# A fused attention, expert and bilinear kernel: the order of its first expert phase, its conversions and its weight buffers changed

## The chip, the cores and the metric

The kernel runs on one core of one Trainium2 chip. A core has five engines that each work through their own list of instructions in order and wait for each other by semaphores: TensorE (PE, matrix products), VectorE (DVE), ScalarE (ACT), GpSimd (POOL) and SyncE (SP), which here only issues transfers. SBUF is the working memory that all engines read, PSUM the banks into which TensorE adds its products. The metric is the time of one execution on the device in microseconds, lower is better.

## What is computed

Three layers follow each other, all in float32.

```python
# 1. attention with decay: B=2, H=8, S=768, D=64, blocks of 64
intra = (q_b @ k_b.T * Dmask) @ v_b
inter = (q_b * lam**(pos+1)) @ kv_state
x[block] = intra + inter              # then x: 1536 x 512
# 2. four experts, each token weighted with p
for e in range(4):
    h = np.maximum(x @ w1[e], 0.0)    # 512 -> 1024
    out += p[:, e:e+1] * (h @ w2[e])  # 1024 -> 512
# 3. bilinear
a = x @ w1; b = x @ w2                # 512 -> 1024 each
y = ((a * b) @ w3) @ w_out            # 1024 -> 1024 -> 512
```

The weights of the third layer come as 64-bit numbers and are turned into float32 on the chip.

## The kernel before

**Precision.** Each float32 operand is split into a high part (rounded, a copy on ScalarE, line 102, names ending in h) and a low part (the difference, a subtraction on VectorE, line 105, names ending in l). A product is then three matmuls: high by low, low by high, high by high (`products`, line 122).

**Stages.** The 1536 tokens are three groups of 512. First comes the attention, with the first expert columns laid between its steps by a list written by hand (`ORDER`). Then **phase one**: for group 0 a loop over the columns k = 8 to 31 (an expert has eight columns of 128 hidden features). Each column is twelve matmuls h, then z (relu times probability, VectorE, line 318, reads the bank of h), hh and hl (its split, lines 325 and 331), and twelve matmuls y of the column k-2. Then **phase two**: groups 1 and 2 together in sixteen chunks m of two columns each, with seven products of sums instead of eight (`multiply`, line 776), for which the weights are summed too (`pair_sums`, lines 682 to 685). Last come the gates and the output.

**What is laid between the columns of phase one.** Calls are put down by `at_step(t, rank, ...)` with a number t = 100 * column + place; `step(t)` issues all that are due, four times a column: after the first six matmuls of h (place 0), after z and hh (25), after half of y (50), after hl (75). Sorting is by t, then by rank. Nothing else sets the order: each engine takes its instructions as they are issued. These are:

- the weights of the column j to come: `prep_high(j)`, `prep_low(j)` (names wh, wl; 1024 wide), in slots s0, s1, ...; a load of the next column is issued when the low part is done with its raw tile;
- the conversion of the 64-bit weights in pieces i = 0 to 23 (w_out 0 to 7, w3 8 to 23; tiles cv): `begin64` (two operations on ScalarE, lines 201 and 205), `bits64` (three on VectorE, lines 211, 215 and 220, then one addition on GpSimd, line 227), `end64` (the split into wo or w3, h and l). The load of the piece i+3 needs the raw tile that the addition of piece i has read;
- `w_block`: W = w3 @ w_out is computed ahead, in one PSUM bank (7): four blocks of six matmuls for each of eight rows kt, then `w_sum` copies the bank (ScalarE, line 614) and `w_store` sends it to DRAM;
- `x_sums` and `x_split`: sums of groups 1 and 2 and their splits, for phase two;
- the early pair sums: `early_load` (line 692) brings the weights of a chunk into a tile of which there is one, `pair_sums` works in it, `early_store` (line 695) sends it to DRAM, from where phase two takes it (t_dram). This is done for the first NPRE chunks; the others make their sums in phase two.

Of the kernel before, what the change touches and what calls it, by code (L numbers as in the profile page):

```python
# [14 lines left out]
P = 128  # L15
# [45 lines left out]
def tile_decay_attention__then__moe_relu__then__bilinear(  # L61
# [73 lines left out]
    def slot_of(j):  # L135
        return j if j < 8 else (j - 8) % 5
# [101 lines left out]
    def end64(i, low):  # L238
# [10 lines left out]
        elif what == "w3":  # L249
            half = q  # L250
            if "w3" not in slots:
                slots["w3"] = pair(1024, "s7", "w3")
            to = slots["w3"]
# [335 lines left out]
    early = ExitStack()  # L589
    wo_p = opened(early, "wo")  # L590
    xs_p = opened(early, "xs")
    ws_p = opened(early, "ws", 2)
    ct_p = opened(early, "ct", 3)
# [5 lines left out]
    def w_block(kt, q, half):  # L599
        if q == 0 and half == 0:  # L600
# [3 lines left out]
                cut("w3", q * 512 + m * P, q * 512 + (m + 1) * P),  # L604
# [42 lines left out]
    NPRE = 8  # L647
# [239 lines left out]
    for j in range(10, NJ):  # L887
        at_step(100 * (j - 3) + 60, 0, None, lambda j=j: prep_high(j))
        at_step(100 * (j - 3) + 76, 0, ("j", j), lambda j=j: prep_low(j))
    for i in range(24):  # L890
        what, n, q, _ = f64[i]
        t = 808 + 95 * i if i < 8 else 1568 + 68 * (i - 8)
        at_step(t, 3, None, lambda i=i: begin64(i))
        at_step(t + 50, 2, None, lambda i=i: bits64(i))
        at_step(t + 75, 9, ("f", i), lambda: None)
        at_step(t + 125, 3, None, lambda i=i: end64(i, False))
        at_step(t + 150, 4, None, lambda i=i: end64(i, True))
        if what == "w3":
            at_step(t + 225, 6, None, lambda n=n, q=q: w_block(n, q, 0))
            at_step(t + 250, 6, None, lambda n=n, q=q: w_block(n, q, 1))  # L900
            if q:
                at_step(t + 251, 1, None, lambda n=n: w_sum(n))
                at_step(t + 325, 9, None, lambda n=n: w_store(n))
    for i, (n, d) in enumerate((n, d) for n in (3, 1, 2, 4) for d in range(2)):
        at_step(1800 + 50 * i, 7, None, lambda n=n, d=d: x_sums(n, d))
    for t, key, src, hi, lo in (
        (2200, "a11", lambda: x_block(0, 0), "xh10", "xh20"),
        (2300, "a12", lambda: x_block(0, 1), "xh11", "xl10"),
        (2400, "a22", lambda: x_block(1, 1), "xh21", "xl20"),
        (2500, "s4", lambda: x_sum[4], "xl11", "xl21"),  # L910
        (2900, "s2", lambda: x_sum[2], "s5h", "s5l"),
        (2925, "s1", lambda: x_sum[1], "s7h", "s7l"),
        (2950, "s3", lambda: x_sum[3], "s6h", "s6l"),
# [3 lines left out]
    for n in range(NPRE):  # L917
        t = 1800 + 120 * n
# [521 lines left out]
```

## Time and profile before

| what | value |
|---|---|
| median of 3 runs | 803.81 us (803.28 to 804.42) |
| profiled execution, its own time | 803.04 us |
| its span from first to last instruction | 801.3 us |
| TensorE busy | 788.7 us (98%) |
| VectorE busy | 554.0 us (69%) |
| ScalarE busy | 332.2 us (41%) |
| GpSimd busy | 148.9 us (19%) |
| mean granted clock of TensorE | 0.998 |

The profile is of one execution. A busy time is the sum of an engine's instructions as the profiler saw them; matmuls overlap each other, so the time from one start to the next says more than the length of one. Idle time of an engine counts only where the engine that ends last waits for it.

### The profile page before, as it was taken

Reading aid. Unit: us, or ns where it says so; the run is one execution under the profiler, and the core shown is the slowest. Engines: PE = TensorE matmul, PEld = TensorE weight load, DVE = VectorE, ACT = ScalarE, POOL = GpSimd, SP = SyncE. Lnnn points to the kernel's source line nnn. Section 1 sums busy time; section 2 is a strip of 40 time slices with the busy share of each in tenths; the row PEclk is TensorE's granted clock in tenths of the full one; section 3 lists DMA queues with packets and bytes.
Section 4 is the critical chain, followed back from the end, with each engine's and each line's share of the span. In section 5 each row is a group of like instructions: output and inputs, shape, how many; then the busy total and the mean of one; then the engine's idle time right before and its main releaser. Section 6 shows DMA issues by size and latency. Waiting matters only on the chain.

```text
span 801.3 us, 10423 instructions
## 1 busy us (share of the span) xinstructions
PE 788.7 (98%) x3968; PEld 645.3 (81%) x3968; DVE 554.0 (69%) x835; ACT 332.2 (41%) x570; POOL 148.9 (19%) x107
## 2 busy tenths in 40 slices
PE   9999999999899999999999999999999999999998
PEld 7777888777777888888888888888888888888887
DVE  7654499998985577667677878787856777677400
ACT  4543256454552465534443334433344442444301
POOL 2112032232220001110001111111100521677000
PEclk9999999999999999999999999999999999999999
DMA  8794356676754165343423232322234201000011
GB/s 268 250 318 141 132 180 198 224 247 207 261 177 148 61 186 175 118 132 114 126 102 106 92 106 93 105 93 92 92 106 145 79 26 54 1 0 1 1 52 53
DMA packets 44418, 101.40 MB, mean 127 GB/s; under 512 B 4944, under 2 KB 10320, under 8 KB 44368
## 3 DMA queue, kind: packets, MB, share of 16 engines
q1 hardware_dynamic: 43696, 100.70, 37.9%
q8 instruction: 31, 0.51, 0.2%
q14 instruction: 19, 0.16, 0.1%
q10 hardware_dynamic: 672, 0.03, 0.1%
HBM read 86.01 MB, written 14.70 MB: 126 GB/s over the span
## 4 chain that ended last, share of the span: by engine, by line
PE 80%; DVE 12%; DMA 5%; issue 1%; ACT 1%; SPq 0%; POOL 0%; ACTq 0%; DVEq 0%; POOLq 0%
PE y L122 27%; PE h L776 19%; PE o L122 8%; PE h L122 5%; PE ab L122 5%; PE a L1236 5%; PE b L1236 5%; DMA w<-in_w_dram 3%; DVE wl L105 2%; PE a L525 2%; PE a L442 2%; DVE hl L331 2%; PE a L519 1%; PE w L122 1%; DVE w3l L105 1%
## 5 line engine op out<-in xcount | busy, mean ns | idle before, releaser
L122 PE MATMUL y<-zp,w 128*128 128x512 f32 x768 | 186.3, 389 | 0.0
L122 PEld LDWEIGHTS y<-zp,w 128*128 128x128 f32 x768 | 144.0, 188 | 30.3 <-ACT ya L855 0.2
L227 POOL TENSOR_TENSOR cv<-cv,raw 128x512 uint32<-128x512 uint32 x40 | 71.3, 1782 | 434.2 <-DVE cv L220 402.2
L796 ACT CAST zp<-z 128x512 fp32r<-128x512 f32 x64 | 39.8, 622 | 107.8 <-DVE z L791 107.8
L325 ACT CAST hh<-z 128x512 fp32r<-128x512 f32 x32 | 19.9, 621 | 106.1 <-DVE z L318 106.1
L122 PE MATMUL o<-w_hi,z 128*128 128x512 f32 (+1 forms) x208 | 60.1, 373 | 0.2 <-DVE z L105 0.2
L800 DVE TENSOR_TENSOR zp<-z,zp 128x512 fp32r<-128x512 f32 x64 | 44.1, 689 | 17.9 <-ACT zp L796 16.5
L105 DVE TENSOR_TENSOR wl<-raw,wh 128x1024 fp32r<-128x1024 f32 (+1 forms) x33 | 41.4, 1253 | 15.8 <-ACT wh L102 15.8
L122 PE MATMUL h<-xl,wh 128*128 128x512 f32 x128 | 51.2, 400 | 0.0
L122 PE MATMUL y<-hl,wh 128*128 128x512 f32 x128 | 50.5, 394 | 0.0
L122 PE MATMUL h<-xh,wl 128*128 128x512 f32 x128 | 50.0, 391 | 0.0
L122 PE MATMUL y<-hh,wl 128*128 128x512 f32 x128 | 49.9, 389 | 0.0
L122 PE MATMUL y<-hh,wh 128*128 128x512 f32 x128 | 49.8, 389 | 0.0
L122 PEld LDWEIGHTS o<-w_hi,z 128*128 128x128 f32 x208 | 37.9, 188 | 7.4 <-DVE z L105 0.5
L789 DVE TENSOR_TENSOR z<-h,v 128x512 f32<-128x512 f32 x16 | 11.0, 690 | 43.5 <-ACT wf L102 29.4
L105 DVE TENSOR_TENSOR w<-w,w 128x512 fp32r<-128x512 f32 x32 | 31.2, 975 | 12.0 <-ACT w L102 12.0
L122 PE MATMUL o<-w_lo,z 128*128 128x512 f32 (+1 forms) x104 | 38.2, 373 | 0.0
L102 ACT CAST wh<-raw 128x1024 fp32r<-128x1024 f32 (+1 forms) x33 | 33.7, 1020 | 9.4 <-PE y L122 5.1
L318 DVE SCALAR_TENSOR_TENSOR z<-h,pb 128x512 f32<-128x512 f32 x32 | 21.9, 685 | 18.8 <-PE h L122 18.3
L122 PE MATMUL h<-xh,wh 128*128 128x512 f32 x128 | 34.8, 390 | 0.0
L791 DVE SCALAR_TENSOR_TENSOR z<-z,pb 128x512 f32<-128x512 f32 x48 | 33.2, 692 | 1.7
L331 DVE TENSOR_TENSOR hl<-z,hh 128x512 fp32r<-128x512 f32 x32 | 28.8, 900 | 5.2 <-ACT hh L325 5.2
(227 smaller groups left out, 1666.9 us busy)
## 6 DMA issues: line engine op xcount, KB each, us to landing
w<-in_w_dram SPq DMA_DIRECT2D x40, 512.0 KB, 4.2
raw<-in_w_dram SPq DMA_DIRECT2D x31, 512.0 KB, 4.4
raw<-in_w3t_dram SPq DMA_DIRECT2D x16, 512.0 KB, 3.3
raw<-in_wab_dram SPq DMA_DIRECT2D x16, 512.0 KB, 3.4
raw<-in_wout_dram SPq DMA_DIRECT2D x8, 512.0 KB, 3.8
t_dram<-w SPq DMA_DIRECT2D x8, 512.0 KB, 3.0
t<-t_dram SPq DMA_DIRECT2D x8, 512.0 KB, 3.7
ab_dram<-cv SPq DMA_DIRECT2D x16, 256.0 KB, 4.2
```

Of the source, the lines that this page charges most:

```text
L102: act.copy(out=hi, in_=src)
L105: eng.tensor_tensor(out=lo, in0=src, in1=hi.bitcast(F32), op=ALU.subtract)
L122: lambda i=i, a=a, b=b: pe.matmul(ps, a, b, start=(first and i == 0), stop=(last and i == n - 1))
L227: pool.tensor_tensor(out=b, in0=b, in1=raws.pop(("f", i))[:, :, 0], op=ALU.add)
L318: dve.scalar_tensor_tensor(out=z, in0=h_ps.pop(k)[0], scalar=0.0, in1=pb_t[k // KF, 0], op0=ALU.max, op1=ALU.mult)
L325: act.copy(out=hh, in_=h_t[k][0])
L331: dve.tensor_tensor(out=hl, in0=z, in1=hh.bitcast(F32), op=ALU.subtract)
L776: pe.matmul(chain_ps[to], w, x, start=begins and j == 0, stop=j == len(seq) - 1, skip_group_check=True,)
L791: dve.scalar_tensor_tensor(out=z, in0=src, scalar=0.0, in1=pb_t[2 * n // KF, PAIR[m]], op0=ALU.max, op1=ALU.mult)
L796: act.copy(out=t[:, 0], in_=z)
L800: dve.tensor_tensor(out=t[:, 1], in0=z_of.pop((m, f)), in1=t[:, 0].bitcast(F32), op=ALU.subtract)
L1236: pe.matmul(t, w, x, start=i == 0 and n in (1, 2, 5), stop=i == len(seq) - 1, skip_group_check=True,)
```

## The change

Pieces are converted in another rhythm, and their bits are issued as the last call of a step, which is the place just ahead of z. Weights of the columns use a ring of four slots instead of five and are prepared one column ahead instead of two. w3 has two slots, for even and odd rows. The sums and splits of x, and the early pair sums, come later, and only four chunks have early pair sums instead of eight. There is one tile for w_sum instead of two, and four tiles for cv instead of three.

```diff
@@ -133,7 +133,7 @@
         return tuple(base.tile([P, n], F32R, tag=f"{tag}{c}", name=f"{name}{c}") for c in "hl")
 
     def slot_of(j):
-        return j if j < 8 else (j - 8) % 5
+        return j if j < 8 else j % 4
 
 
     f64 = [("wo", mt, mt // 4, wout[mt]) for mt in range(KF)]
@@ -248,9 +248,10 @@
             to = slots["wo", n // 2]
         elif what == "w3":
             half = q
-            if "w3" not in slots:
-                slots["w3"] = pair(1024, "s7", "w3")
-            to = slots["w3"]
+            key = "w3", n % 2
+            if key not in slots:
+                slots[key] = pair(1024, f"s{(4, 7)[n % 2]}", "w3")
+            to = slots[key]
         hi, lo = (t[:, half * 512 : half * 512 + 512] for t in to)
         if low:
             low_part(singles.pop(i), hi, lo)
@@ -589,8 +590,8 @@
     early = ExitStack()
     wo_p = opened(early, "wo")
     xs_p = opened(early, "xs")
-    ws_p = opened(early, "ws", 2)
-    ct_p = opened(early, "ct", 3)
+    ws_p = opened(early, "ws")
+    ct_p = opened(early, "ct", 4)
     xt_p = opened(early, "xt")
     r64_p = opened(early, "r64", 3)
     w_ps, w_part = {}, {}
@@ -601,7 +602,7 @@
             w_ps[kt] = bank(7, "w")
         pairs = [
             (
-                cut("w3", q * 512 + m * P, q * 512 + (m + 1) * P),
+                cut(("w3", kt % 2), q * 512 + m * P, q * 512 + (m + 1) * P),
                 cut(("wo", 2 * q + m // 2), m % 2 * DM, (m % 2 + 1) * DM),
             )
             for m in range(4)
@@ -644,7 +645,7 @@
 
     PAIR = (1, 2)
     NP = NJ // 2
-    NPRE = 8
+    NPRE = 4
     PAIRS = 100 * NJ
     GATES = PAIRS + 100 * (NP + 1)
     x_sum, x_own = {}, {}
@@ -885,37 +886,37 @@
 
 
     for j in range(10, NJ):
-        at_step(100 * (j - 3) + 60, 0, None, lambda j=j: prep_high(j))
-        at_step(100 * (j - 3) + 76, 0, ("j", j), lambda j=j: prep_low(j))
+        at_step(100 * (j - 2) + 76, 0, None, lambda j=j: prep_high(j))
+        at_step(100 * (j - 1) + 1, 0, ("j", j), lambda j=j: prep_low(j))
     for i in range(24):
         what, n, q, _ = f64[i]
-        t = 808 + 95 * i if i < 8 else 1568 + 68 * (i - 8)
+        t = 800 + 100 * min(i, 11) + 57 * max(i - 11, 0)
         at_step(t, 3, None, lambda i=i: begin64(i))
-        at_step(t + 50, 2, None, lambda i=i: bits64(i))
-        at_step(t + 75, 9, ("f", i), lambda: None)
-        at_step(t + 125, 3, None, lambda i=i: end64(i, False))
-        at_step(t + 150, 4, None, lambda i=i: end64(i, True))
+        at_step(t + (100 if i < 12 else 75), 9, None, lambda i=i: bits64(i))
+        at_step(t + (125 if i < 12 else 100), 9, ("f", i), lambda: None)
+        at_step(t + 150, 3, None, lambda i=i: end64(i, False))
+        at_step(t + 175, 4, None, lambda i=i: end64(i, True))
         if what == "w3":
-            at_step(t + 225, 6, None, lambda n=n, q=q: w_block(n, q, 0))
-            at_step(t + 250, 6, None, lambda n=n, q=q: w_block(n, q, 1))
+            at_step(t + 325, 6, None, lambda n=n, q=q: w_block(n, q, 0))
+            at_step(t + 350, 6, None, lambda n=n, q=q: w_block(n, q, 1))
             if q:
-                at_step(t + 251, 1, None, lambda n=n: w_sum(n))
-                at_step(t + 325, 9, None, lambda n=n: w_store(n))
+                at_step(t + 351, 1, None, lambda n=n: w_sum(n))
+                at_step(t + 425, 9, None, lambda n=n: w_store(n))
     for i, (n, d) in enumerate((n, d) for n in (3, 1, 2, 4) for d in range(2)):
-        at_step(1800 + 50 * i, 7, None, lambda n=n, d=d: x_sums(n, d))
+        at_step(2200 + 40 * i, 7, None, lambda n=n, d=d: x_sums(n, d))
     for t, key, src, hi, lo in (
-        (2200, "a11", lambda: x_block(0, 0), "xh10", "xh20"),
-        (2300, "a12", lambda: x_block(0, 1), "xh11", "xl10"),
-        (2400, "a22", lambda: x_block(1, 1), "xh21", "xl20"),
-        (2500, "s4", lambda: x_sum[4], "xl11", "xl21"),
-        (2900, "s2", lambda: x_sum[2], "s5h", "s5l"),
-        (2925, "s1", lambda: x_sum[1], "s7h", "s7l"),
-        (2950, "s3", lambda: x_sum[3], "s6h", "s6l"),
+        (2540, "a11", lambda: x_block(0, 0), "xh10", "xh20"),
+        (2620, "a12", lambda: x_block(0, 1), "xh11", "xl10"),
+        (2700, "a22", lambda: x_block(1, 1), "xh21", "xl20"),
+        (2780, "s4", lambda: x_sum[4], "xl11", "xl21"),
+        (2950, "s2", lambda: x_sum[2], "s5h", "s5l"),
+        (3000, "s1", lambda: x_sum[1], "s7h", "s7l"),
+        (2975, "s3", lambda: x_sum[3], "s6h", "s6l"),
     ):
         at_step(t, 7, None, lambda k=key, s=src, hi=hi, lo=lo: x_split(k, s(), hi, lo, False))
         at_step(t + 25, 7, None, lambda k=key, s=src, hi=hi, lo=lo: x_split(k, s(), hi, lo, True))
     for n in range(NPRE):
-        t = 1800 + 120 * n
+        t = 2400 + 110 * n
         if n == 0:
             at_step(t - 75, 8, None, lambda: early_load(0))
         at_step(t, 8, None, lambda n=n: pair_sums(n))
```

The first place is VectorE in the columns 14 to 16. The names: cv the piece in conversion, wo, hl and wl low parts, z as above. Before, from the z of column 14 to that of column 15:

```order
L318 SCALAR_TENSOR_TENSOR z<-h,pb 128x512
L211 TENSOR_SCALAR cv<-cv 128x512
L215 TENSOR_SCALAR cv<-cv 128x512
L220 SCALAR_TENSOR_TENSOR cv<-raw_1359,cv 128x512
L105 TENSOR_TENSOR wo<-cv,wo 128x512
L331 TENSOR_TENSOR hl<-z,hh 128x512
L105 TENSOR_TENSOR wl<-raw,wh 128x1024
L318 SCALAR_TENSOR_TENSOR z<-h,pb 128x512
```

In the change, from the bits ahead of the z of column 15 to the z of column 16:

```order
L211 TENSOR_SCALAR cv<-cv 128x512
L215 TENSOR_SCALAR cv<-cv 128x512
L220 SCALAR_TENSOR_TENSOR cv<-raw_1376,cv 128x512
L319 SCALAR_TENSOR_TENSOR z<-h,pb 128x512
L105 TENSOR_TENSOR wl<-raw,wh 128x1024
L332 TENSOR_TENSOR hl<-z,hh 128x512
L105 TENSOR_TENSOR wo<-cv,wo 128x512
L211 TENSOR_SCALAR cv<-cv 128x512
L215 TENSOR_SCALAR cv<-cv 128x512
L220 SCALAR_TENSOR_TENSOR cv<-raw_1424,cv 128x512
L319 SCALAR_TENSOR_TENSOR z<-h,pb 128x512
```

The three lines of bits (L211, L215, L220) stood behind z, with wo and hl next; now they stand ahead of z, and wl, of the next column, stands right behind it, ahead of hl and wo.

The second place is ScalarE around two of the copies w_sum. Before, around the copy for row kt = 4:

```order
L102 CAST a22h<-xf_89 128x1024
L325 CAST hh<-z 128x512
L614 COPY w_sum<-w 128x512
L102 CAST w3h<-cv 128x512
L201 ACTIVATE cv<-raw_2126 128x512
L205 ACTIVATE raw_2126<-raw_2126 128x512
L102 CAST wh<-raw 128x1024
```

In the change, around the copies for the rows kt = 4 and 5:

```order
L201 ACTIVATE cv<-raw_2201 128x512
L205 ACTIVATE raw_2201<-raw_2201 128x512
L615 COPY w_sum<-w 128x512
L326 CAST hh<-z 128x512
L102 CAST w3h<-cv 128x512
L102 CAST a12h<-xf_87 128x1024
L102 CAST wh<-raw 128x1024
L102 CAST w3h<-cv 128x512
L102 CAST a22h<-xf_89 128x1024
L326 CAST hh<-z 128x512
L615 COPY w_sum<-w 128x512
L102 CAST w3h<-cv 128x512
```

Before, this w_sum stands right behind an hh; in the change that of kt = 4 stands behind the two operations of a conversion, and that of kt = 5 behind an hh.

The third place is SyncE, which issues the stores of w_sum. Before, from the store of one pair sum to the next store of w_sum:

```order
L695 DMA t_dram<-w_2038 128x1024
L154 DMA raw_2126<-in_w3t_dram 128x1024
L692 DMA w_2143<-in_w_dram 128x2x512
L617 DMA w_dram<-w_sum 128x512
L163 DMA raw<-in_w_dram 128x1024
```

In the change, near the same point of the phase:

```order
L163 DMA raw<-in_w_dram 128x1024
L696 DMA t_dram<-w_2144 128x1024
L154 DMA raw_2201<-in_w3t_dram 128x1024
L618 DMA w_dram<-w_sum 128x512
L693 DMA w_2243<-in_w_dram 128x2x512
L163 DMA raw<-in_w_dram 128x1024
L696 DMA t_dram<-w_2243 128x1024
L618 DMA w_dram<-w_sum 128x512
```

In both, a store of w_sum stands behind a store of a pair sum (t_dram) and behind a load for the conversion; in the change w_sum has one tile, so that the next copy waits for this store.

## Rows read from the trace of the kernel before

**Rows 1.** The page, busy time of TensorE and its share of the span.

```profile
PE 788.7 (98%) x3968; PEld 645.3 (81%) x3968; DVE 554.0 (69%) x835; ACT 332.2 (41%) x570; POOL 148.9 (19%) x107
```

**Rows 2.** Windows of 20 us: window, length, busy by engine, granted clock, DMA.

```profile
120.00:140.00 20.00, 20.00 (x90) 16.53 (x90) 19.72 (x28) 12.29 (x20) 5.76 (x4) 1.00 0.61 199
...
200.00:220.00 20.00, 18.01 (x80) 14.55 (x78) 19.34 (x29) 10.02 (x16) 4.91 (x3) 1.00 0.81 259
...
220.00:240.00 20.00, 18.84 (x76) 15.46 (x77) 17.34 (x24) 10.99 (x17) 5.15 (x3) 0.91 0.51 178
```

**Rows 3.** What TensorE's matmuls waited for: total us, times, longest.

```profile
PE w L122 <- ACT w_sum L614: 5.2, 3, 3.2
PE w L122 <- DVE w3l L105: 1.9, 2, 1.5
```

**Rows 4.** Timeline, VectorE: the z of column 8 and of column 31 (start, us).

```profile
96.90 0.69 DVE L318 SCALAR_TENSOR_TENSOR z<-h,pb 128x512 f32<-128x512 f32 x1
...
276.03 0.69 DVE L318 SCALAR_TENSOR_TENSOR z<-h,pb 128x512 f32<-128x512 f32 x1 [3.37 <-PE h L122]
```

**Rows 5.** The chain that ended last, in order of time: start, us, what.

```profile
96.86 2.72 PE y L122 x12
```

**Rows 6.** Groups by form, 86 to 280 us; last GpSimd's additions, min/median/max ns.

```profile
L331 DVE TENSOR_TENSOR hl<-z,hh 128x512 fp32r<-128x512 f32 x25 | 23.9, 956 | 3.6 <-ACT hh L325 3.6
L105 DVE TENSOR_TENSOR w3l<-cv,w3h 128x512 fp32r<-128x512 f32 x16 | 19.0, 1188 | 2.9 <-ACT w3h L102 2.9
L318 DVE SCALAR_TENSOR_TENSOR z<-h,pb 128x512 f32<-128x512 f32 x25 | 17.1, 684 | 12.1 <-PE h L122 11.9
...
L227 POOL TENSOR_TENSOR cv<-cv,raw x24: 1283/1545/2077, 100.8 to 242.0; 128x512 uint32<-128x512 uint32 x24
```

**Rows 7.** Timeline, 139 us: GpSimd's addition and the hl beside it.

```profile
139.13 1.55 POOL L227 TENSOR_TENSOR cv<-cv,raw 128x512 uint32<-128x512 uint32 x1 [3.44 <-DVE cv L220]
139.42 1.81 DVE L331 TENSOR_TENSOR hl<-z,hh 128x512 fp32r<-128x512 f32 x1
```

**Rows 8.** Timeline, 208 us: z behind the bits, the addition, a 1024-wide low part.

```profile
208.21 0.69 DVE L220 SCALAR_TENSOR_TENSOR cv<-raw,cv 128x512 uint32<-128x512 uint32 x1
208.82 0.68 DVE L318 SCALAR_TENSOR_TENSOR z<-h,pb 128x512 f32<-128x512 f32 x1
...
209.13 1.30 POOL L227 TENSOR_TENSOR cv<-cv,raw 128x512 uint32<-128x512 uint32 x1 [5.30 <-DVE cv L220]
...
209.42 2.10 DVE L105 TENSOR_TENSOR a12l<-xf,a12h 128x1024 fp32r<-128x1024 f32 x1
213.56 0.69 DVE L220 SCALAR_TENSOR_TENSOR cv<-raw,cv 128x512 uint32<-128x512 uint32 x1
```

**Rows 9.** Timeline, column 9: the first y matmul and z.

```profile
102.14 0.39 PE L122 MATMUL y<-hl,wh 128*128 128x512 f32 x1
102.34 0.69 DVE L318 SCALAR_TENSOR_TENSOR z<-h,pb 128x512 f32<-128x512 f32 x1 [0.65 <-PE h L122]
```

**Rows 10.** Timeline: hh, w_sum and the W matmul after the longest pause.

```profile
220.01 0.62 ACT L325 CAST hh<-z 128x512 fp32r<-128x512 f32 x1 [4.65 <-DVE z L318]
220.53 0.58 ACT L614 COPY w_sum<-w 128x512 f32<-128x512 f32 x1
...
221.16 0.80 PE L122 MATMUL w<-wol,w3h 128*128 128x512 f32 x1 [3.15 <-ACT w_sum L614]
```

**Rows 11.** Stores of w_sum: issues, KB, median us to landing; all: min/median/max.

```profile
w_dram<-w_sum SPq DMA_DIRECT2D x7, 256.0 KB, 4.9
...
DMA to landing us min/median/max: 3.2/4.6/6.3
```

**Rows 12.** Timeline, ScalarE: first copies of chunks 3, 7 and 15, phase two.

```profile
330.82 0.59 ACT L783 COPY v<-h 128x512 f32<-128x512 f32 x1 [0.83 <-PE h L776]
...
412.42 0.59 ACT L783 COPY v<-h 128x512 f32<-128x512 f32 x1 [3.82 <-PE h L776]
...
576.83 0.59 ACT L783 COPY v<-h 128x512 f32<-128x512 f32 x1 [2.98 <-PE h L776]
```

## The prediction

> **What bounds the kernel now.** I began with the busy time by engine: TensorE is busy for 788.7 of 801.3 us [rows 1], so whatever can be won is what TensorE loses, and I looked for where it loses it. The table of 20-us windows answers that: from 20 to 140 us it is busy for all 20 us of a window, between 140 and 260 us it is not (18.01 and 18.84 us in the two windows shown), and in one of them the granted clock is 0.91, which means that some of that window ran at 1.2 instead of 2.4 GHz [rows 2]. Those windows are the second half of phase one, in which the conversions of w3, the W blocks, the sums and splits of x and the early pair sums are laid between the expert columns. The waits of TensorE name two causes only: the copy that empties the bank of W (w_sum, on ScalarE) and the low part of w3 (on VectorE) [rows 3].
>
> How much it loses follows from the work alone. Twelve matmuls take 2.72 us [rows 5], six 1.36; a column issues 24 of them (12 for h, 12 for y), 5.44 us. From the z of column 8 to the z of column 31, 276.03 - 96.90 = 179.1 us pass [rows 4]. In them lie 23 columns (125.1 us) and 32 W blocks of six matmuls (43.5 us), together 168.6 us. So **10.5 us** of phase one are pauses, restarts and half clock: the most that this change can win there.
>
> Why the pauses come: VectorE is busy for 17 to 20 us of a window from 100 to 240 us (19.72, 19.34, 17.34 in those shown) [rows 2]. Part of this is not work. An hl takes 956 ns in the mean and a w3l 1188 [rows 6], where the same 512 elements need 0.69 us when nothing is beside them. The reason is visible in one iteration: GpSimd's addition of the conversion runs from 139.13 to 140.68, and the hl that starts at 139.42 ends at 141.23, 0.55 us after it [rows 7]. A VectorE operation with two operands in SBUF stands still while GpSimd adds. z does not: one of its operands is a PSUM bank, and its mean is 684 ns [rows 6], also where the addition runs through it [rows 8]. The late VectorE then makes z late, ScalarE stands at hh for z (4.65 us idle before 220.01), w_sum is queued right behind that hh, and TensorE waits 3.15 us for it [rows 10].
>
> **The change part by part.**
>
> *Conversion bits beside z.* Before, the bits stand behind z, and hl, wo or w3l run into the addition: 1.81 instead of 0.69 us, 1.12 us in each of 24 conversions. Behind the change, in columns 9 to 18, the order is wl, hl, wo, bits, z. One stretch of before has nearly this order, and it gives the price: L220 at 208.21, z at 208.82, the addition 209.13 to 210.43, the 1024-wide low part from 209.42 to 211.52, L220 again at 213.56 [rows 8]. That is a VectorE cycle of 5.35 us when z follows at once, just under TensorE's 5.44. When z must wait for TensorE anyway, the addition is over before wl starts, and the cycle has about 0.9 us more room. So VectorE keeps up with TensorE there, at no cost.
>
> *Weights prepared one column ahead instead of two (ring of four).* wl(k+1) now stands behind z(k). z starts 0.20 us after TensorE's first y matmul of that column (102.14 and 102.34) [rows 9], wl starts 0.61 later and takes 1.2, so it ends 2.0 us after that y matmul; with the addition in its way as in [rows 8], 2.70 us behind z, 2.9 us. The second matmul of h(k+1), the first that reads wl, comes after 12 y matmuls and one more: 2.72 + 0.23 = 2.95 us. I cost it at nothing: the cover is the 2.72 us of y. From column 19 on the W blocks lengthen the cover by 1.36 us each.
>
> *Sums and splits later, four pair sums fewer, second w3 slot.* A pair sum is one operation as wide as an hl and three of half that width, some 1.9 us by the 0.69 of an hl; four of them leave phase one. I added VectorE's operations column by column for 19 to 27 from the order (z, hl, w3l, xs about 0.6 each, 1024-wide ones 1.14, bits 1.5, a pair sum 1.6, 1.1 for each operation that still runs into an addition): 77 us against 86 us of TensorE (nine columns and their 27 W blocks). No column is over by more than 1.2 us, and those that are have two or more W blocks as cover. A w3l now ends a column and a half before its block instead of three quarters, so the 1.9 us of w3l waits [rows 3] go.
>
> *One buffer for w_sum instead of two, and the order around the hand-overs.* This is where I leave a rest. Seven times the bank of W passes from one row of blocks to the next; four times only six matmuls (1.36 us) lie between, and w_sum needs some 0.85 of these: 0.63 from its start to TensorE's next matmul (220.53 to 221.16 [rows 10]) and the 0.2 of [rows 9] from a matmul to its reader. w_sum must now wait until the store of the one before has landed. Three of these stores stand in SyncE's queue behind a store of t (the early pair sums), which waits for VectorE; a store of w_sum takes 3.2 to 6.3 us to land, 4.9 in the middle of this phase [rows 11]. I estimate, counting on from the start of z with the durations above: in columns 24, 25 and 26 the store is issued some 4 to 7 us into the column and lands at about 8, 11 and 12 us, when w_sum is wanted at 8.4, 9.7 and 11.1. Each of the three can cost from 0 to 2 us; I take 1.3 us for all.
>
> *Phase two gets four more pair sums.* Chunks 3 to 6 take the form of chunks 7 to 14. From 330.82 to 412.42 four chunks without sums take 20.40 us each, from 412.42 to 576.83 eight with them take 20.55 [rows 12]. Four times 0.15 is 0.6 us more. The transfers that go (four stores, four loads of t) lie beside other work.
>
> **The sum.** 801.3 - 10.5 + 1.3 + 0.6 = 792.7 us of span. The profiled execution took 803.04 us, 1.7 more than its span, so 794.5; it is 0.8 us under the median of the runs, 803.81. Forecast: **795.2 us**, 8.6 us or 1.1% faster.
>
> **One rule beside the rows.** The Trainium skill, "SBUF — State Buffer", section "Who interferes with whom", has the shared port pair as an exclusive lock: the loser blocks for the whole instruction. Taken to its end, wl blocks in every column, as in the first rival; the forecast stands on the 0.9 us of room that the trace leaves.
>
> **The rivals.**
> - *wl too late.* If the bits end only just before z in columns 9 to 18, wl runs into the addition. With the 1.30 us addition of [rows 8] it ends at 2.9 us, a pause of about 0.1 in each of ten columns; with the longest GpSimd additions (2.08 us [rows 6]) the pause is 0.9. That is 1 to 9 us: 796 to 803. Against it: once z waits for TensorE, the bits get further ahead with each column.
> - *The stores of w_sum hold TensorE more than I take.* With two of three spots at 2 us and a colder clock after, 3 to 6 us: 797 to 801.
> - *Slower: all seven hand-overs wait.* Place: w_sum behind the one buffer and behind conversions that wait for their loads. The three waits of before average 1.74 us (5.2 over three) [rows 3]; the gain is 9.9 us after phase two's 0.6, so 1.4 us at each of seven brings no change and above 1.65 us the kernel is slower than before by 0.2%. At the 3.15 us of the worst one [rows 10] all seven would give 22 us: 816. Against it: three hand-overs have 2.72 us or more of cover, and only one w_sum with short cover still stands right behind an hh.
> - *The change doesn't do what it says.* The additions run into other operations (hl, xs) and the pauses stay, in other places: 803 to 805. Against it: at least 12 of the 24 additions fall beside z, and some 8 us of VectorE work leave the phase.
>
> **How the numbers follow.** Forecast (793.3 to 797) 0.60; more at the w_sum stores 0.18; wl late 0.08; no change 0.07; slower 0.07. The range of 8 in 10 reaches from all pauses gone with phase two's price halved (793.3) into the second and first rivals: 800.3. A measurement of this kernel can tell about 0.2%, 1.6 us, from no change. Faster than 802.2: 0.60 + 0.18 + most of 0.08, 0.86; within 0.2%: 0.07; slower than 805.4: 0.07.
>
> **What would show it.** Right: the windows from 140 to 260 us show TensorE at 20.00 with clock 1.00; the z of column 31 stands 170 us after that of column 8 (168.6 at best); hl and w3l have means below 0.9 us; the w3l waits are gone, and what remains of the w_sum waits is under 2 us; chunks 3 to 6 last 20.55 us. Wrong: TensorE waits on wl in columns 9 to 18, or w_sum waits on its own store more than three times, or VectorE still waits long for the loads of the early pair sums.

## The result: 0.9% faster, in the range, with one term of the sum too small

The changed kernel took 796.21 us (median of four runs, 796.16 to 796.46), the kernel before 803.54 (median of four, three of them the runs of the table above): a ratio of 0.9911 [0.9894, 0.9929]. The forecast was 795.2, from 793.3 to 800.3. The profiled execution took 796.46 us with a span of 794.7.

The page's busy time by engine, after (for [rows 1]):

```profile
PE 786.7 (99%) x3968; PEld 644.1 (81%) x3968; DVE 547.2 (69%) x835; ACT 333.5 (42%) x570; POOL 142.7 (18%) x107
```

TensorE's busy time fell by 2.0 us and the span by 6.6, so most of what went was waiting. The windows of 20 us, after, with the columns of [rows 2]:

```profile
140.00:160.00 20.00, 20.00 (x90) 16.57 (x89) 16.93 (x26) 12.28 (x19) 5.23 (x4) 1.00 0.53 197
...
180.00:200.00 20.00, 18.86 (x84) 15.28 (x82) 17.48 (x27) 9.80 (x16) 4.64 (x4) 1.00 0.59 200
200.00:220.00 20.00, 19.76 (x87) 16.37 (x88) 18.15 (x29) 11.54 (x18) 4.37 (x3) 1.00 0.68 221
220.00:240.00 20.00, 18.82 (x84) 15.21 (x83) 18.49 (x26) 8.06 (x12) 4.38 (x3) 1.00 0.59 187
```

Phase one is full up to 180 us; what is left lies between 180 and 240, and the clock is 1.00 throughout. What TensorE waited for, after (for [rows 3]):

```profile
PE w L122 <- ACT w_sum L615: 2.6, 2, 1.4
```

The waits for w3l are gone and two for w_sum remain. VectorE's timeline, after, the z of column 8 and of column 31 (for [rows 4]):

```profile
96.90 0.69 DVE L319 SCALAR_TENSOR_TENSOR z<-h,pb 128x512 f32<-128x512 f32 x1 [6.27 <-PE h L122]
...
268.74 0.69 DVE L319 SCALAR_TENSOR_TENSOR z<-h,pb 128x512 f32<-128x512 f32 x1 [1.88 <-PE h L122]
```

They are 171.84 us apart: 7.3 less than before, and 3.2 above the 168.6 of work. Two groups by form, after (for [rows 6]):

```profile
L332 DVE TENSOR_TENSOR hl<-z,hh 128x512 fp32r<-128x512 f32 x25 | 19.3, 773 | 1.5 <-ACT hh L326 1.5
...
L105 DVE TENSOR_TENSOR w3l<-cv,w3h 128x512 fp32r<-128x512 f32 x16 | 14.3, 892 | 0.1
```

Both became shorter, as expected; whether that is where the time came from is for the experiments to say. ScalarE's first copies of chunks 3, 7 and 15, after (for [rows 12]):

```profile
323.53 0.59 ACT L784 COPY v<-h 128x512 f32<-128x512 f32 x1 [0.83 <-PE h L777]
...
405.77 0.59 ACT L784 COPY v<-h 128x512 f32<-128x512 f32 x1 [2.99 <-PE h L777]
...
570.31 0.59 ACT L784 COPY v<-h 128x512 f32<-128x512 f32 x1 [3.05 <-PE h L777]
```

Chunks 3 to 6 now take 82.24 us, 20.56 each, as chunks 7 to 14 do: 0.64 us more in all. So 7.29 - 0.64 = 6.65, which is the 6.6 of the span.

The chain that ended last, after, around the two pauses:

```profile
191.35 1.23 DVE wl L105
...
192.59 0.33 SPq L163
...
193.45 6.07 DMA w_dram<-w_sum
...
199.60 0.59 ACT w_sum L615
...
200.24 1.65 PE w L122 x6
...
218.75 5.38 DMA w_dram<-w_sum
...
224.21 0.59 ACT w_sum L615
...
224.85 1.67 PE w L122 x6
```

Two copies w_sum in ScalarE's timeline, after, those of the rows kt = 1 and 2:

```profile
185.30 0.59 ACT L615 COPY w_sum<-w 128x512 f32<-128x512 f32 x1 [1.06 <-PE w L122]
...
199.60 0.58 ACT L615 COPY w_sum<-w 128x512 f32<-128x512 f32 x1 [4.02 <-DMA w_dram<-w_sum]
```

Read the chain backwards from 199.60. The copy of row kt = 2 waits for the store of kt = 1 to land; that store needs 6.07 us and was issued at 193.45, though its tile had been copied at 185.30. In SyncE's list it stood behind the load of the next column's weights (line 163), which waits for a wl. The six matmuls behind each pause take 1.65 and 1.67 us instead of 1.36. The 20-us windows lose 1.14 + 0.24 + 1.18 = 2.6 us, the slower restarts 0.6: that is the 3.2.

### The profile page after: what moved, and what is told of

Same layout as the page of the kernel before. It is cut to its first block, busy times and chain, and to the rows that moved or that the text cites. A ratio compares the mean times of both kernels' runs of the same rounds, so it can differ in the third digit from the quotient of the medians.

```text
span 794.7 us, 10384 instructions
## 1 busy us (share of the span) xinstructions
PE 786.7 (99%) x3968; PEld 644.1 (81%) x3968; DVE 547.2 (69%) x835; ACT 333.5 (42%) x570; POOL 142.7 (18%) x107
## 4 chain that ended last, share of the span: by engine, by line
PE 96%; DMA 2%; ACT 1%; DVE 0%; issue 0%; SPq 0%; ACTq 0%
PE y L122 33%; PE h L777 19%; PE h L122 11%; PE o L122 8%; PE ab L122 5%; PE a L1237 5%; PE b L1237 5%; PE w L122 5%; PE a L526 2%; PE a L443 2%; DMA w_dram<-w_sum 1%; PE a L520 1%; DMA kv<-in_kv_dram 1%; PE a L483 1%; DVE ab L1085 0%
## 5 line engine op out<-in xcount | busy, mean ns | idle before, releaser
L227 POOL TENSOR_TENSOR cv<-cv,raw 128x512 uint32<-128x512 uint32 x40 | 65.5, 1636 | 433.5 <-DVE cv L220 391.7
L105 DVE TENSOR_TENSOR wl<-raw,wh 128x1024 fp32r<-128x1024 f32 (+1 forms) x33 | 39.8, 1207 | 3.4 <-ACT wh L102 3.4
L105 DVE TENSOR_TENSOR w<-w,w 128x512 fp32r<-128x512 f32 x32 | 35.6, 1112 | 4.9 <-ACT w L102 4.9
L201 ACT ACTIVATE cv<-raw 128x512 f32<-128x512 f32 x40 | 26.8, 670 | 9.2 <-DMA raw<-in_w3t_dram 5.7
```

Source lines behind the costliest of these rows:

```text
L105: eng.tensor_tensor(out=lo, in0=src, in1=hi.bitcast(F32), op=ALU.subtract)
L201: act.activation(out=singles[i], in_=raws["f", i][:, :, 1].bitcast(F32), func=ACTF.Abs)
L227: pool.tensor_tensor(out=b, in0=b, in1=raws.pop(("f", i))[:, :, 0], op=ALU.add)
```

## The experiments

Each kernel was timed in turn with the kernel before on the same chip; the ratio is to that one. "z distance" is the start of the z of column 31 less that of column 8 in the profiled execution (before 179.1, after 171.84, work alone 168.6). It is a better gauge than the span, because the attention ahead of it moved the z of column 8 between 96.7 and 98.4 us from run to run. But it is of one execution of each kernel, and says nothing of how far executions differ; the ratio does.

### What carries the gain

**Pair sums alone.** The kernel before with one number changed.

```diff
-    NPRE = 8
+    NPRE = 4
```

> The kernel before with one part of the change alone: four early pair sums instead of eight. Theory (the bits are the larger part, the pair sums the smaller): the last of the three pauses at w_sum goes or shrinks, the earlier ones stay; phase two is 0.6 us longer; 800.5 to 803. Rival (the work taken from VectorE is what counts): all pauses behind 205 us go, 797 to 799.

Measured: 796.67 us, ratio 0.9934 [0.9922, 0.9946], z distance 172.12. TensorE's waits, and the hl group, of this kernel:

```profile
PE w L122 <- DVE w3l L105: 1.5, 1, 1.5
PE w L122 <- ACT w_sum L614: 1.0, 1, 1.0
```

```profile
L331 DVE TENSOR_TENSOR hl<-z,hh 128x512 fp32r<-128x512 f32 x25 | 23.9, 955 | 3.6 <-ACT hh L325 3.6
```

The additions block hl exactly as before (955 ns against 956), and still most of the gain is there: 7.0 of the 7.3 us of z distance. My view of the cause falls here, though not for every pause. The kernel before has five: at 151.60, 178.86, 198.86, 221.16 and 249.86 us (1.47, 1.05, 0.44, 3.15 and 1.03 us of waiting). The last three, which have a pair sum in the queue ahead of what TensorE waits for, are gone here, and the first two are left, at 151.85 and 179.10. By the trace, the first of these comes from blocked conversions, though no run tried that alone. Before, the z of column 16 and the pause:

```profile
142.29 0.68 DVE L318 SCALAR_TENSOR_TENSOR z<-h,pb 128x512 f32<-128x512 f32 x1
...
151.60 0.50 PE L122 MATMUL w<-woh,w3l 128*128 128x512 f32 x1 [1.47 <-DVE w3l L105]
```

From column 10 to column 16 the z of the kernel before stand 5.59 us apart and none of them waits for TensorE, whose columns take 5.44; each cycle holds a low part that runs beside an addition (1.81 us instead of 0.69, or 2.34 instead of 1.22 where it is a wl). The z of column 8 starts at 96.90 in both kernels, that of column 16 at 142.29 before and at 140.42 in the change. The first pair sum runs only at 157.05, behind this pause.

**Bits alone.** The kernel before with the bits, and what hangs on them, moved to the place ahead of z.

```diff
-        at_step(t + 50, 2, None, lambda i=i: bits64(i))
-        at_step(t + 75, 9, ("f", i), lambda: None)
-        at_step(t + 125, 3, None, lambda i=i: end64(i, False))
-        at_step(t + 150, 4, None, lambda i=i: end64(i, True))
+        tb = (t + 149) // 100 * 100
+        at_step(tb, 9, None, lambda i=i: bits64(i))
+        at_step(tb + 25, 9, ("f", i), lambda: None)
+        at_step(max(t + 125, tb + 25), 3, None, lambda i=i: end64(i, False))
+        at_step(max(t + 150, tb + 50), 4, None, lambda i=i: end64(i, True))
```

> The kernel before with one part of the change alone: the bits of a conversion wait for the next place just ahead of z, the split 25 and 50 places behind. If either half frees VectorE: hl and wl means near those of an operation alone in columns 9 to 16, the early pauses (w3l at 150, w_sum at 178 us) go, 0.992 to 0.996 of before. If the pair sums alone hold the phase: 0.997 or more, with the pauses behind 180 us as before.

Measured: 812.75 us, ratio 1.0121 [1.0105, 1.0138], z distance 187.59. hl and w3l were unblocked (means 688 and 686 ns), and the kernel is slower. Most of it is one wait:

```profile
PE w L122 <- ACT w3h L102: 10.9, 2, 9.4
```

VectorE now takes the bits of two pieces in a row ahead of one z, and the first W block waits 9.4 us for a w3h that stands behind the hh of this z. Neither of the two outcomes expected came. With its W blocks left in their old places, this kernel doesn't price the bits by themselves. It shows that a shorter hl saves nothing when something else is late.

**All of the change, but the bits behind z again.**

```diff
-        at_step(t + (100 if i < 12 else 75), 9, None, lambda i=i: bits64(i))
-        at_step(t + (125 if i < 12 else 100), 9, ("f", i), lambda: None)
+        at_step(t + 50, 2, None, lambda i=i: bits64(i))
+        at_step(t + 75, 9, ("f", i), lambda: None)
```

> The changed kernel with one part undone: the bits of a conversion stand 50 places behind its beginning again, so behind z and wl and ahead of hl or w3l; all else as changed. Theory (additions that run into hl and w3l are the loss): hl and w3l go back to means near 1.0 and 1.2 us, VectorE's cycle in columns 9 to 18 becomes 5.59 against TensorE's 5.44 us, and the time is 1.5 to 5 us above the changed kernel: 797.7 to 801. Rival (the gain is from fewer pair sums, the second w3 slot and the later splits): within 0.8 us of the changed kernel, 795.4 to 797.

Measured: 799.7 us, ratio 0.9974 [0.9964, 0.9985], z distance 175.15; hl stayed at 774 ns (773 in the change), since the additions now hit other operations (w3l has 1033 ns in the mean, 892 in the change). The chain behind the second of its two pauses:

```profile
209.27 1.56 POOL cv L227
...
210.85 0.33 SPq L154
211.23 5.18 DMA w_dram<-w_sum
...
216.49 0.59 ACT w_sum L615
```

The loss of 3.3 us of z distance against the change came through SyncE: here the store of w_sum stands behind a conversion load, and that load waits for the addition. In the first pause, at 201.05, the store stands behind the load of weights, as in the change, and that load waits for a wl which runs beside an addition (2.11 us instead of 1.22). So a blocked operation of VectorE does cost here, by way of SyncE's list. The edit also issues the conversion loads earlier, so it undoes more than the place of the bits. This looked like a confirmation of the bits; the last experiment below, where the queue holds nothing up, shows that their place costs nothing there.

**The pair sums' time without their transfers.** The kernel before with NPRE 4, and four more pair sums in the old places that work on one tile, loaded once and never stored. Their result isn't used.

```diff
-    NPRE = 8
+    NPRE = 4
...
+    at_step(1800 + 120 * 3 + 60, 9, None, idle_load)
+    for n in range(4, 8):
+        at_step(1800 + 120 * n, 8, None, lambda: pair_sums("idle"))
```

> The kernel before with four early pair sums and the rest of their work kept on VectorE: at the old places it makes four pair sums in a tile that is loaded once and not stored; nothing reads them. VectorE's order is that of the kernel before, only the loads, the stores and the waits for them are gone. If VectorE's time is what four pair sums cost, the pauses behind 190 us come back: the two z 177 us apart or more, 0.998 of before or more. If the wait for the one tile's load and store is what they cost, it stays near the run with four alone (172.1 us apart, 0.993). In between: the share of each.

Measured: 802.23 us, ratio 1.000 [0.9989, 1.0011], z distance 177.05: by the ratio the gain is gone again. VectorE's timeline there (the last of the sums and z), then ScalarE's:

```profile
215.02 1.79 DVE L105 TENSOR_TENSOR w3l<-cv,w3h 128x512 fp32r<-128x512 f32 x1
216.74 0.68 DVE L682 TENSOR_TENSOR w<-w 128x512 f32<-128x512 f32 x1
...
218.59 0.69 DVE L318 SCALAR_TENSOR_TENSOR z<-h,pb 128x512 f32<-128x512 f32 x1
```

```profile
219.31 0.62 ACT L325 CAST hh<-z 128x512 fp32r<-128x512 f32 x1 [4.25 <-DVE z L318]
219.83 0.58 ACT L614 COPY w_sum<-w 128x512 f32<-128x512 f32 x1
```

This is the pause of [rows 10] again. z has no idle time before it: VectorE comes to it straight from the four operations of a pair sum (1.85 us) and, ahead of them, a w3l beside an addition (1.79), ScalarE stands 4.25 us at hh, and w_sum is behind hh. What the pair sums cost is above all VectorE's time in the queue ahead of z: NPRE 4 alone won 7.0 us of z distance, and the sums' time alone takes 4.9 of them back. The other 2.1 would be the part of their loads and stores: the pauses at 198.86 and 249.86, where in the kernel before a pair sum stands 1.18 and 2.01 us for its load, did not come back. That part was not tried by itself.

**The change with eight early pair sums.** They have to start earlier, to fit.

```diff
-    NPRE = 4
+    NPRE = 8
...
-        t = 2400 + 110 * n
+        t = 1960 + 110 * n
```

> The changed kernel with one part undone: eight early pair sums instead of four, the four more in columns 19 to 22. The run with four pair sums alone in the kernel before took nearly all of the gain, so two theories: the pair sums hold phase one whatever the rest is (then pauses of 4 us or more come back and the time is 0.996 of before or more), or VectorE had too much of two kinds of loss and either half of the change frees it (then this run keeps most of the gain, 0.990 to 0.995 of before, phase two 0.6 us shorter).

Measured: 807.13 us, ratio 1.0048 [1.0036, 1.006], z distance 182.02. TensorE's longest waits, and VectorE ahead of the worst:

```profile
PE h L122 <- DVE wl L105: 4.4, 2, 3.8
PE w L122 <- ACT w_sum L615: 4.3, 2, 2.8
```

```profile
187.03 0.69 DVE L683 TENSOR_TENSOR w<-w 128x512 f32<-128x512 f32 x1 [4.62 <-DMA w<-in_w_dram]
...
190.10 0.69 DVE L319 SCALAR_TENSOR_TENSOR z<-h,pb 128x512 f32<-128x512 f32 x1
190.70 1.22 DVE L105 TENSOR_TENSOR wl<-raw,wh 128x1024 fp32r<-128x1024 f32 x1
```

A pair sum stands 4.62 us for its load, ahead of z, and wl stands behind z. One column ahead, a late z takes wl with it, and TensorE waits 3.8 us; before, wl was made for a column further on. So the four kernels read together:

| ratio to before | old order | new order |
|---|---|---|
| 8 early pair sums | 1 | 1.0048 |
| 4 early pair sums | 0.9934 | 0.9911 |

The new order costs 0.5% with eight sums (which start at place 1960 there, 1800 in the kernel before) and gives about 0.2% with four, which the intervals do not separate from none. Behind that 0.2% lie four pauses: with four sums the old order has those at 151.85 and 179.10 (1.47 and 1.05 us); the new order has neither of them, but those at 200.24 and 224.85 (1.38 and 1.18).

### The cover of wl

**wl behind hl**, some 1.4 us later, in the changed kernel.

```diff
-        at_step(100 * (j - 1) + 1, 0, ("j", j), lambda j=j: prep_low(j))
+        at_step(100 * (j - 1) + 51, 0, ("j", j), lambda j=j: prep_low(j))
```

> The changed kernel with the low part of the next column's weights one step later, so that it stands behind hl instead of ahead of it. hl waits for hh, so wl ends about 3.5 us after the first y matmul of the column instead of 2.0, and the second matmul of h wants it at 2.95. If the 2.72 us of y are the cover, as the prediction has it, TensorE waits for wl about 0.6 us, with the restart 0.7, in each of the columns 9 to 18 and less often later: 5 to 8 us more, 801 to 804. If there is more cover than this, no wait on wl and 796 to 797.

Measured: 812.15 us, ratio 1.0132 [1.0112, 1.0152], z distance 187.49, 15.65 more than the change. TensorE's waits and the first of them in the timeline:

```profile
PE h L122 <- DVE wl L105: 12.6, 16, 2.3
```

```profile
105.54 0.50 PE L122 MATMUL h<-xh,wl 128*128 128x512 f32 x1 [0.41 <-DVE wl L105]
```

The cover is as short as it was counted, and the price was more than expected (15.65 us, not 5 to 8): the first ten waits, of 0.35 to 0.41 us, make 3.7 us, and six later ones, of up to 2.29 us, another 8.9. The prediction had wl ending 2.0 us after the first y matmul and wanted at 2.95, a margin of 0.95; wl begins 1.43 us later here, so it should be 0.48 late, and TensorE waits 0.41. In the change no wait for wl is left, so the term at nothing was right.

### What holds the rest

**The store at once.** In the changed kernel, the store of w_sum is issued right behind its copy.

```diff
-                at_step(t + 425, 9, None, lambda n=n: w_store(n))
+                at_step(t + 352, 9, None, lambda n=n: w_store(n))
```

> The changed kernel with one call moved: the store of w_sum is issued in the step of the copy instead of some 75 places later. In the changed kernel two pauses of TensorE are left in phase one (1.38 and 1.21 us by its waits, 3.2 us with what the restart costs by the time between the z of columns 8 and 31). Theory (one tile for w_sum whose store is issued late in the queue): both pauses go, the distance of the two z falls from 171.8 to under 169.5 us and the time from 796.2 to 793.0 to 793.7. Rival (the hand-over of the bank is too short, or ScalarE is held by conversions that wait for loads): the pauses stay or move, 795.5 to 797.

Measured: 795.39 us, ratio 0.9921 [0.9909, 0.9934], z distance 170.14: 1.7 less than the change. By the ratio the two can't be told apart, and the expected time of under 793.7 did not come. The pause at 200 is gone, the one near 223 stays. SyncE, then ScalarE there:

```profile
216.76 0.32 SPq L696 DMA_DIRECT2D t_dram<-w  x1
217.17 0.38 SPq L154 DMA_DIRECT2D raw<-in_w3t_dram  x1
```

```profile
221.22 0.67 ACT L201 ACTIVATE cv<-raw 128x512 f32<-128x512 f32 x1 [3.79 <-DMA raw<-in_w3t_dram]
...
222.34 0.57 ACT L615 COPY w_sum<-w 128x512 f32<-128x512 f32 x1
```

This pause has another cause than the chain named: the conversion's load stands behind the store of a pair sum in SyncE's list, ScalarE waits 3.79 us for it, and w_sum is behind that conversion.

**Two tiles for w_sum** in the changed kernel, paid for with one of cv, whose splits are moved forward.

```diff
-    ws_p = opened(early, "ws")
-    ct_p = opened(early, "ct", 4)
+    ws_p = opened(early, "ws", 2)
+    ct_p = opened(early, "ct", 3)
...
-        at_step(t + 150, 3, None, lambda i=i: end64(i, False))
-        at_step(t + 175, 4, None, lambda i=i: end64(i, True))
+        at_step(t + (150 if i < 12 else 125), 3, None, lambda i=i: end64(i, False))
+        at_step(t + (175 if i < 11 else 165 if i == 11 else 150), 4, None, lambda i=i: end64(i, True))
```

> The changed kernel with two tiles for w_sum as before and, for the space, three for cv; the splits of pieces 11 to 23 come 10 to 25 places earlier so that three tiles suffice. Theory (the single tile is what holds w_sum): the waits on the store are gone, 793.0 to 794.0. Rival (bank hand-over or conversions): 795.5 to 797. If the three cv tiles hold ScalarE, a wait of cv on w3l shows up and the time stays above 795.

Measured: 796.61 us, ratio 0.9934 [0.9922, 0.9946], z distance 171.40. No store holds w_sum now, and two pauses remain: at 223.62 it stands behind the same load as above (ScalarE waited 3.57 us for it), at 211.32 behind a conversion that waited for a cv tile, of which this kernel took one away. So it neither confirms nor refutes the price of the single tile; it does show that the second pause is not the tile's.

**The conversion's load ahead of the pair sum's store**, added to the store at once.

```diff
-        at_step(t + (125 if i < 12 else 100), 9, ("f", i), lambda: None)
+        at_step(t + (125 if i < 12 else 85), 9.5, ("f", i), lambda: None)
```

> The changed kernel with the store of w_sum issued at once (as in the first experiment) and, for pieces 12 to 23, the load of the piece i+3 issued 15 places earlier, which puts the last of these loads ahead of the store of a pair sum in SyncE's queue. In the first experiment one pause is left (1.2 us at 223 us); the copy stands behind a conversion there whose load was issued at 218.3 us behind such a store. Theory (ScalarE is held by that load): the pause goes, the two z are under 169.2 us apart, the time is about 1.2 us below the first experiment, 0.990 to 0.991 of before. Rival (the bank's hand-over with 1.36 us of cover is too short by itself): the pause stays near 1.2 us.

Measured: 795.3 us, ratio 0.9899 [0.9886, 0.9911], z distance 170.37. The pause at 223 is gone and one of the same size is there at 236, which is why the distance didn't move. VectorE, then ScalarE:

```profile
227.77 1.47 DVE L683 TENSOR_TENSOR w<-w 128x512 f32<-128x512 f32 x1 [0.62 <-DMA w<-in_w_dram]
...
234.27 0.68 DVE L319 SCALAR_TENSOR_TENSOR z<-h,pb 128x512 f32<-128x512 f32 x1
```

```profile
234.98 0.62 ACT L326 CAST hh<-z 128x512 fp32r<-128x512 f32 x1 [4.50 <-DVE z L319]
235.51 0.58 ACT L615 COPY w_sum<-w 128x512 f32<-128x512 f32 x1
```

The same figure for a third time: a pair sum late and long (0.62 us of waiting, and 1.47 instead of 0.69), z late, hh late, and behind it the w_sum of kt = 5. Here the pair sum does not stand straight ahead of z: w3l, a12l, hl and the bits lie between, without a gap. That the sum is what counts is shown only by the run below that moves it.

**Six early pair sums** in that kernel (NPRE 6).

> The same, with six early pair sums instead of four; the two more fall into columns 28 and 29, where VectorE has little else. If VectorE's room decides, phase one stays as in that kernel and phase two loses two of its four longer chunks, 0.3 us faster. Rival (each pair sum brings its own wait for the one tile and its store and load): pauses come back, slower by 0.5 us or more.

Measured: 795.28 us, ratio 0.9898 [0.9886, 0.9911], z distance 170.55. No difference that can be told: phase two has two chunks less to pay for (0.3 us), and the wait for w_sum is 0.2 longer.

**The last two pair sums later**, added to the load ahead (with four sums).

```diff
-        t = 2400 + 110 * n
+        t = (2400, 2510, 2720, 2830)[n]
```

> The kernel with the store of w_sum at once and the conversion loads ahead, and now the third and fourth early pair sum one column later (places 2720 and 2830 instead of 2620 and 2730). In that kernel one pause is left (1.4 us at 234 us): the copy stands behind an hh, z is late because the third pair sum and its wait for the load fall into a column that VectorE just fills. Theory: the pause goes, the two z stand 168.6 to 169.1 us apart and the time is 0.987 to 0.989 of before. Rival (the pause belongs to the hand-over with 1.36 us of cover): it stays, 0.990.

Measured: 793.25 us, ratio 0.9892 [0.9876, 0.9908], z distance 168.64. That is the 168.6 of the work alone: phase one has no pause left. It has the lowest time of all: 2.1 us under the store at once, with the kernel before at nearly the same time beside both (801.88 and 801.97). Against the change itself the intervals of the ratios overlap; that it is faster rests on the z distance, 3.2 us less, in one execution of each. Against four pair sums alone (0.9934 [0.9922, 0.9946]) they do not overlap: with these three places mended, the rest of the change is worth some 0.4%, and 3.5 us of z distance, which is what the two early pauses cost. Which of its parts takes these away was not tried one by one.

**The bits behind z, in that kernel.**

```diff
-        at_step(t + (100 if i < 12 else 75), 9, None, lambda i=i: bits64(i))
+        at_step(t + 50, 2, None, lambda i=i: bits64(i))
```

> The kernel of the first experiment of this group (store at once, loads ahead, sums later) with the bits behind z and wl, 50 places after the beginning of the conversion, as in the experiment that undid the bits in the changed kernel and cost 3.5 us there. Two theories on these: the additions that run into hl and w3l make VectorE late (then 2 to 4 us over the first of this group again), or VectorE has room for them and what was late was the raw load behind the later addition and with it the store of w_sum in SyncE's queue (then within 1 us of the first of this group).

Measured: 793.45 us, ratio 0.9895 [0.988, 0.9909], z distance 168.67: no difference, though in the columns 10 to 14 the z stand 5.57 to 5.59 us apart again. The first W matmul comes at 156.4 us here, at 149.7 in the kernel before, so the lateness meets no W block. The windows from column 8 on, of the kernel with the bits beside z, then with the bits behind it:

```profile
97.00:180.00 83.00, 83.00 (x368) 68.72 (x367) 66.40 (x101) 48.69 (x75) 20.05 (x15) 1.00 0.52 182
180.00:260.00 80.00, 80.00 (x355) 66.24 (x354) 65.07 (x91) 37.58 (x55) 13.39 (x9) 1.00 0.55 180
```

```profile
97.00:180.00 83.00, 83.00 (x368) 68.70 (x367) 76.39 (x102) 48.84 (x75) 23.54 (x15) 1.00 0.53 183
180.00:260.00 80.00, 80.00 (x355) 66.26 (x354) 65.67 (x91) 37.65 (x55) 13.61 (x9) 1.00 0.53 179
```

The blocked conversions are real: VectorE is busy 10 us longer in the first window. But 76.4 of 83 us still leaves room, and TensorE is busy for every microsecond of both. In the second window, where the three later pauses of the kernel before lay, the place of the bits changes VectorE's time by 0.6 us.

## Why the prediction was right, and where it was not

**The total and the bound.** 10.5 us as the most that phase one can give was right to the tenth: the kernel with no pause left has a z distance of 168.64. The forecast came out 1.0 us low. With a rest of 3.2 instead of 1.3 the sum gives an own time of 794.4 + 1.9 = 796.3 (792.7 and 1.7 make 794.4, not the 794.5 that was written); measured were 796.46. The 0.8 us added for the median were not there this time (796.21). That the time lies below 797 is luck in part: a rest of 3.2 us is what the second rival stated (3 to 6), and with the 0.8 us it would have been 797.1. Of the signs, three did not come: TensorE is not at 20.00 in every window, the z are 171.84 us apart and not 170, and 2.6 us of waits for w_sum are left, not under 2.

**The step that failed: "Why the pauses come", and with it the part "Conversion bits beside z" as the source of the gain.** The rows were read rightly, 1.12 us of standing still in each of 24 conversions, but the inference from them holds only for the early pauses: for that at 151.60 the trace has the 5.59 us of VectorE's cycle ahead of it, and for that at 178.86 it is not shown (a w3l beside an addition, 1.80 us, stands ahead of z there, and a pair sum some 7 us further ahead). A mean over the phase says that VectorE loses time, not that it loses it ahead of the operation that TensorE waits for. The pair sums alone give 0.9934 with hl still at 955 ns, and the bits' place is worth nothing in the best kernel, where W begins later. Right was the second half of that paragraph: late z, late hh, w_sum behind hh. In the pause of [rows 10] what made z too late were the four operations of a pair sum straight ahead of it: without them, a w3l of 1.80 us still stands ahead of that z, and there is no pause.

**"Sums and splits later, four pair sums fewer"** thus carried the gain. In the prediction it was one count among several (77 us of VectorE's work against 86 of TensorE's). The conclusion was right (in the kernel without a pause VectorE is busy for 73.3 of the 85.7 us from the z of column 19 to that of column 28), but the pair sums were given no price of their own: the 10.5 us were put down to all parts together.

**"One buffer for w_sum" was the mis-sized term**: 1.3 us, measured 3.2. The mechanism, a late store, was right for both pauses, but the copy in column 23, which stood idle 4.02 us for a store, was not on the list of three: I looked at the stores behind pair sums and not at one behind a load of weights. The other pause, in column 26, was on the list and has a second cause that ends at nearly the same time: the store landed at 224.13, and the conversion ahead of w_sum, late by its load (issued at 218.31, landed 4.5 us later), starts its two operations at 222.86 and would hold w_sum until about 224. So the store at once and the second tile both leave that pause as it was.

**"Weights prepared one column ahead" at nothing** was right, and the cover is as thin as stated: wl behind hl costs 15.65 us. The first rival, wl blocked in every column as the Trainium skill's rule of the shared port ("SBUF — State Buffer", "Who interferes with whom") would have it at its end, did not come: no wait names wl, which takes 1250 ns in the mean. The rule agrees with the rows of blocked operations (an hl of 1.81 us beside an addition, 0.69 without), and decides nothing here.

**Phase two** cost 0.64 us, forecast 0.6. The slower rival (all hand-overs wait) did not come: two waited, 1.3 us each.

**Still open:** what the bits' place would be worth in the kernel before, had its W blocks been moved back with them; and which part of the change takes away the two early pauses. Neither was tried.

## What to carry to other kernels

An engine that loses time on the mean need not lose it at the one place where it counts: follow the chain from the pause back to the operation that stands straight ahead of the late one, and take that away alone before giving credit to a whole change, and do so pause by pause, since two pauses of one phase can have two causes. In a queue that is worked in order, a store stands best right behind what it stores, and a load that others wait for stands ahead of stores that wait. Several hidden limits stand behind each other, and each one removed shows the next at nearly the same time: here the first and the third that went gave 1.7 us of z distance each, and the second nothing until the third was gone too.

## What the hardware showed unexpectedly

GpSimd's addition also holds up a VectorE operation with one SBUF operand and a constant, where I had named those with two. In the kernel with the bits alone, VectorE's line 215, which takes 0.43 us elsewhere, beside an addition:

```profile
155.24 1.28 POOL L227 TENSOR_TENSOR cv<-cv,raw 128x512 uint32<-128x512 uint32 x1 [5.74 <-DVE cv L220]
155.38 1.42 DVE L215 TENSOR_SCALAR cv<-cv 128x512 uint32<-128x512 uint32 x1
```

The addition ran from 155.24 to 156.52, and L215 ended 0.28 us after it; five of the 24 L215 in that kernel took 1.42 to 1.45 us. The next addition, at 157.76, ran beside a z, which took 0.68. And a pause costs TensorE more than its wait: the six matmuls behind one took 1.65 and 1.67 us in place of 1.36, 0.3 us on top of waits of 1.2 to 1.4.
